# Half of w_in kept on chip until its split, half through DRAM once, and matmul operands moved to multiples of 2 KB

## The chip, the cores and the metric

The kernel runs on one core of a Trainium2 chip. The metric is the device time of one execution in microseconds. The engines are named as in the profile: PE (TensorE matmul, PEld its weight loads), DVE (VectorE), ACT (ScalarE), POOL (GpSimd) and SP (SyncE, which issues most DMAs).

## The reference

Three layers follow one another, all in f32 (some of the 64-bit inputs are cut to f32 on the chip).

```
attention, B=8, H=8, S=576, D=64: k and v pooled over 8 rows (72 keys);
  attn = softmax(q k_p^T / 8);  x = attn v_p, as 4608 tokens x 512
experts: e = argmax(x w_gate); gate = softmax(x w_gate)[e]; eom = sigmoid(x w_output_gate)
  x = gate * eom[e] * (relu(x w1[e]) w2[e])         8 experts, 512 -> 1024 -> 512
dense:   h = x w_in                                  512 -> 2048
         out = (s * relu(h)^2 + b) w_out             2048 -> 512
```

The change concerns w_in, 512 x 2048, and the places of the tiles that PE reads.

## The kernel before

**Precision.** Matmuls of the experts and of the dense layer run on f32r operands. To keep f32 accuracy an operand is split into hi (ACT: a copy that rounds, L800) and lo (DVE: the rest, L801), by `split`, and each product is three matmuls: hi hi, hi lo, lo hi.

**Stages.** Attention runs to about 222 us, the experts to about 742, the dense layer from 749.8 to the end. The experts go slot by slot (128 tokens of one expert, 39 slots here): `l1` (L996, 24 matmuls, weights xh and xl, moving operand wa), a transpose, `l2` (L1025, 24 matmuls, moving operand wb). In each slot the function `side` also calls `db.step`, which prepares the dense layer's weights. The dense layer runs over 9 groups of 512 tokens, and in each over 16 blocks f of 128 hidden units: `c1(g, f)` (L1222, 12 matmuls, weights a block of 128 columns of wa or wb, moving operand xdh and xdl), relu on ACT, square and affine on DVE, a split into gh (ACT) and gl (DVE), and two steps later `c2(g, f)` (L1251, four times 3 matmuls, one for each 128 tokens j, weights gh and gl, moving operand wo[f]) into the four accumulators po0 to po3. After the last f of a group `store` copies each po to a yo tile (ACT for even, DVE for odd tokens' blocks) and POOL sends it out by an indirect DMA. A step below is one c1 and one c2: 24 matmuls. Program order on each engine is the order written; nothing is reordered.

**w_in and w_out.** They come in as 64-bit numbers. `Doubles` turns them into f32 in 64 pieces of 128 rows by 256 columns: a load (SP), then in `step` (L909) a pipeline of three calls per piece over ACT, DVE and POOL, whose last operation is POOL's add (L938), and a split. Pieces 0 to 11 and 44 to 63 are w_out's, 12 to 43 w_in's. The first 44 run beside the experts; the last 20 of w_out in steps 1 to 11 of dense group 0, two a step. A split piece of w_out goes to the wo tiles. A split piece of w_in, hi and lo, is stored to two DRAM tensors wi (64 stores of 128 KB), since wa and wb hold the experts' weights until the end of the experts. Then `reload` (L1371) brings them back into wa (columns 0 to 1023, in `tail`, 8 DMAs, 4 MB) and wb (columns 1024 to 2047, in steps 0 to 3 of group 0, two DMAs of 512 KB each).

**tail** (L1414) runs ahead of the last l2: it frees the experts' raw weights, opens the pool of xdh and xdl in their place, issues the reload of wa and the first two loads of w_out, and cuts (splits) the four slices of group 0's input.

**Places.** Pools on the left grow upward from the constants, two pools on the right downward from the top. On the left wa begins at byte 22464 of each partition, which is 11 x 2048 - 64; every later tile there that PE reads as f32r (wb, wo, xh, xl, hh, hl, gh, gl) begins at a multiple of 2 KB less 64 bytes too, since all sizes from there on are multiples of 1 KB. On the right the raw weights, and after them xdh and xdl, begin at a multiple of 2 KB less 32 bytes (xdh at 196576 = 96 x 2048 - 32). A slice of weights is 128 columns, 512 bytes, a moving operand 512 columns, 2 KB.

Of the kernel before, what the change touches and what calls it, by code (L numbers as in the profile page):

```python
# [8 lines left out]
F32 = mybir.dt.float32  # L9
F32R = mybir.dt.float32r  # L10
BF16 = mybir.dt.bfloat16
F16 = mybir.dt.float16
I32 = mybir.dt.int32
# [3 lines left out]
ALU = mybir.AluOpType  # L17
# [9 lines left out]
DM = H * D  # L27
E = 8
FE = 1024
FF = 2048  # L30
P = 128
# [767 lines left out]
def split(nc, hi, lo, raw, eng=None):  # L799
    nc.scalar.activation(out=hi, in_=raw, func=AF.Copy)  # L800
    (eng or nc.vector).tensor_tensor(out=lo, in0=raw, in1=hi.bitcast(F32), op=ALU.subtract)  # L801
# [60 lines left out]
CW = 256  # L862
# [7 lines left out]
class Doubles:  # L870
# [3 lines left out]


    def __init__(self, tc, ctx, w_in, w_out, wi):
        self.nc, self.tc = tc.nc, tc
        self.p3 = ctx.enter_context(tc.tile_pool(name="db3", bufs=3))
        self.wi, self.wo = wi, []
        self.more(ctx, EARLY * CW // DM)  # L880
        self.src = [w.bitcast(I32) for w in (w_out, w_in)]
        out = [(0, r, c) for r in range(FF // P) for c in range(DM // CW)]
        self.pieces = out[:EARLY] + [(1, r, c) for c in range(FF // CW) for r in range(DM // P)] + out[EARLY:]
        self.x, self.t, self.stores = {}, {}, []
        self.run(0, EARLY + len(self.pieces) // 2)
# [23 lines left out]
    def step(self):  # L909
        nc, n = self.nc, self.n  # L910
        if n == self.end + 3:
            return
        self.n += 1
        while self.stores:
            d, t = self.stores.pop(0)
            nc.sync.dma_start(out=d, in_=t)
        self.load(n + AHEAD)
        if n < self.end:
            x = self.x[n]
            t = self.p3.tile([P, CW], I32, tag="dt", name="dt", bufs=4)  # L920
            self.t[n] = t
            lo = x[:, :, 0]
            nc.scalar.activation(out=lo, in_=lo.bitcast(U32), func=AF.Copy, scale=2.0 ** -29)  # L923
            nc.vector.tensor_single_scalar(out=t, in_=x[:, :, 1], scalar=0x7FFFFFFF, op=ALU.bitwise_and)
            nc.gpsimd.tensor_scalar(
                out=t.bitcast(F32), in0=t.bitcast(F32), scalar1=LO64, scalar2=HI64, op0=ALU.max, op1=ALU.min
            )
        m = n - 1
        if self.begin <= m < self.end:
            x, t = self.x[m], self.t[m]  # L930
            nc.vector.tensor_scalar(
                out=t, in0=t, scalar1=3, scalar2=0x3FFFFFFF,
                op0=ALU.logical_shift_left, op1=ALU.bitwise_and,
            )
            nc.vector.scalar_tensor_tensor(  # L935
                out=t, in0=x[:, :, 1], scalar=-0x40000000, in1=t, op0=ALU.bitwise_and, op1=ALU.bitwise_or
            )
            nc.gpsimd.tensor_tensor(out=t, in0=t, in1=x[:, :, 0], op=ALU.add)  # L938
        m = n - 2
        if self.begin <= m < self.end:  # L940
            x, f = self.x.pop(m), self.t.pop(m).bitcast(F32)
            w, r, c = self.pieces[m]
            if w == 0:
                hi, lo = [o[:, c * CW:(c + 1) * CW] for o in self.wo[r]]
            else:
                hi = x.rearrange("p c w -> p (c w)")[:, 0:CW].bitcast(F32R)
                lo = f.bitcast(F32R)
            split(nc, hi, lo, f)
            if w == 1:
                for d, s in zip(self.wi, (hi, lo)):  # L950
                    self.stores.append((d[:, r, c * CW:(c + 1) * CW], s.bitcast(F32)))


def experts(ctx, tc, c, kp, wt, xd, ys, wide, side, ahead, tail):
# [212 lines left out]
class Dense:  # L1167
# [43 lines left out]
    def run(self, ctx, reload):  # L1211
        nc, tc, xs, gs, po, s_b = self.nc, self.tc, self.xs, self.gs, self.po, self.s_b
        db = self.db
# [49 lines left out]
                store(GT * g + j, o)  # L1263

        def store(t, src):
            y = p3.tile([P, DM], F32, tag="yo", name="yo", bufs=4)
            if t % 2:
                nc.vector.tensor_copy(out=y, in_=src)
            else:
                nc.scalar.copy(out=y, in_=src)  # L1270
            nc.gpsimd.indirect_dma_start(  # L1271
                out=self.out[:, :], out_offset=bass.IndirectOffsetOnAxis(ap=self.tok.to[:, t:t + 1], axis=0),
                in_=y, in_offset=None,
            )
# [5 lines left out]
        for n in range(len(steps)):  # L1280
            nxt = None
            g, f = steps[n]
            if g > 0 and g + 1 < NGRP and f % 2 == 0:
                k = f % 8 // 2
                if f < 8:
                    self.load(g + 1, k)
                else:
                    self.join(g + 1, k, [nc.gpsimd, nc.gpsimd])
                    nxt = g + 1, k
            if g == 0 and REST < f <= REST + 4:  # L1290
                nxt = 1, f - REST - 1
                self.join(*nxt, [nc.scalar, nc.vector])
            rest = g == 0 and 1 <= f <= REST
            c1(g, f, db.step if rest else None)
            if rest:
                db.step()
            if g == 0:
                if f < 4:
                    reload(f)
                if f == REST:  # L1300
                    for k in range(4):
                        self.load(1, k)
            if LAG <= n < len(steps) - END + LAG:
                g, f = steps[n - LAG]
                for j in range(GT):
                    c2(g, f, f + 1, j)
            if nxt is not None:
                self.cut(*nxt)
# [5 lines left out]
def kernel(  # L1314
# [15 lines left out]
    nc = tc.nc  # L1330
    ctx.enter_context(tc.manual_schedule())
    c = constants(tc, ctx, nc)
# [12 lines left out]

    ys = dram.tile([N + P, 2 * DM], U16, name="ys")
    tok = Tokens(nc, kpool, dram.tile([N, 2], I32, name="tab"), dram.tile([N, 1], F32, name="gsd"))
    wi = [dram.tile([P, DM // P, FF], F32, name=f"wi{i}") for i in range(2)]

    wt = Experts(tc, moe_w1, moe_w2, kpool)  # L1350
    raw = ExitStack()
    for i in range(2):
        wt.open_raw(i, raw.enter_context(tc.tile_pool(name=f"raw{i}", bufs=1, side="right")))
# [14 lines left out]
        attention(x, tc, c, q, k, v, moe_w_gate, moe_w_output_gate, xd, lg, ro, hooks)  # L1368
    wt.open_b(ctx.enter_context(tc.tile_pool(name="wb", bufs=1)))

    def reload(i, f0, f1):  # L1371
        for m, w in enumerate((wt.a, wt.b)[i]):
            nc.sync.dma_start(
                out=w.bitcast(F32).rearrange("p (k f) -> p k f", f=FE)[:, :, f0:f1],
                in_=wi[m][:, :, FE * i + f0:FE * i + f1],
            )

    db = Doubles(tc, ctx, moe2_w_in, moe2_w_out, wi)

# [31 lines left out]
                dn.join(0, k, [nc.scalar, nc.vector])  # L1411

    with ExitStack() as x:
        def tail():  # L1414
            raw.close()
            dn.open(ctx.enter_context(tc.tile_pool(name="dn2", bufs=2, side="right")))
            reload(0, 0, P)
            reload(0, P, 2 * P)
            db.run(db.end, len(db.pieces))
            reload(0, 2 * P, 4 * P)  # L1420
            reload(0, 4 * P, FE)
            for k in range(4):
                dn.cut(0, k)

        experts(x, tc, c, kp, wt, xd, ys, wide, side, ahead, tail)
    dn.run(ctx, lambda j: reload(1, 2 * P * j, 2 * P * (j + 1)))


_INS = [
# [23 lines left out]
```

## Time and profile before

| | us |
|---|---|
| median of 3 runs | 1573.66 |
| lowest, highest | 1565.76, 1579.52 |
| the profiled execution, own time | 1566.95 |
| its span (first to last instruction) | 1565.3 |
| PE busy | 1500.5 (96%) |
| DVE, ACT, POOL busy | 817.2, 527.9, 491.3 |

The span is what the profile covers; its own time includes 1.65 us around it. Busy times of engines overlap. A matmul's duration in the profile includes the way through the array, so it is longer than the distance from one start to the next; the distance is what counts, and it is read from starts.

### The profile page before, as it was taken

The numbers are of one execution on the slowest core, as the hardware profiler recorded it, in microseconds if no ns is written. First come the engines' busy times: TensorE is split into PE (matmuls) and PEld (weight loads), VectorE is DVE, ScalarE is ACT, GpSimd is POOL, SyncE is SP. The second block draws the span as 40 slices with busy tenths as digits, with TensorE's granted clock in tenths as the row PEclk, the third lists the DMA queues.
The fourth block names the chain that finished last, engine by engine and source line by source line (L and its number), as shares of the span: only waits on it lengthen the run. The fifth ranks groups of instructions, "written<-read, shape, count | busy, mean of one in ns | idle before, by whom it ended". The sixth has DMA issues, their size and how long they took to land.

```text
span 1565.3 us, 21155 instructions
## 1 busy us (share of the span) xinstructions
PE 1500.5 (96%) x7280; PEld 1226.6 (78%) x7280; DVE 817.2 (52%) x1516; ACT 527.9 (34%) x1017; POOL 491.3 (31%) x521
## 2 busy tenths in 40 slices
PE   5998999999989999998999999999999999999997
PEld 4876878887768887886887888888888888888885
DVE  6688775576644657433695434343444434444332
ACT  3554524254433345222343222222222222222221
POOL 6745222355554454500460304040220404040000
PEclk8999999999989999999999999999999999999999
DMA  8975244255744647492923101010010101000000
GB/s 243 262 233 150 82 135 176 69 185 156 235 164 104 204 132 235 132 83 57 308 71 77 28 14 41 21 41 21 27 34 14 35 14 41 14 27 1 23 5 27
DMA packets 139592, 153.56 MB, mean 98 GB/s; under 512 B 62078, under 2 KB 96126, under 8 KB 139454
## 3 DMA queue, kind: packets, MB, share of 16 engines
q1 hardware_dynamic: 123918, 101.83, 23.4%
q0 software_dynamic: 15536, 50.12, 10.3%
q8 instruction: 59, 0.97, 0.3%
q14 instruction: 79, 0.65, 0.2%
HBM read 104.93 MB, written 37.54 MB: 91 GB/s over the span
## 4 chain that ended last, share of the span: by engine, by line
PE 46%; DVE 3%; DMA 1%; ACT 1%; SPq 1%; issue 1%; POOLq 0%; DVEq 0%; ACTq 0%
PE po L1259 8%; PE ph L1228 8%; PE ph L1230 8%; PE ph L1229 8%; PE po L1261 8%; PE po L1260 7%; DVE gl L1248 1%; DVE r L1234 1%; DMA dx<-in_moe_w_out 1%; DVE r L1233 0%; PE py L1034 0%; DVE wo L801 0%; DVE dt L935 0%; ACT dx L923 0%; DVE dy L1201 0%
## 5 line engine op out<-in xcount | busy, mean ns | idle before, releaser
L1233 DVE TENSOR_TENSOR r<-r 128x512 f32<-128x512 f32 x144 | 104.9, 728 | 320.8 <-ACT r L1232 320.6
L1271 POOL DMA_INDIRECT out<-yo,kp_pos x36 | 35.7, 991 | 604.0 <-ACT yo L1270 523.2
L1259 PE MATMUL po<-wo,gh 128*128 128x512 f32 x560 | 221.9, 396 | 0.0
L1261 PE MATMUL po<-wo,gl 128*128 128x512 f32 x560 | 219.8, 393 | 0.0
L1260 PE MATMUL po<-wo,gh 128*128 128x512 f32 x560 | 218.1, 389 | 0.0
L1034 PE MATMUL py<-wb,hh 128*128 128x512 f32 x624 | 196.1, 397 | 10.8 <-ACT wb L800 6.2
L1232 ACT ACTIVATE r<-ph 128x512 f32<-128x512 f32 x144 | 85.9, 597 | 342.8 <-PE ph L1230 342.8
L1245 ACT ACTIVATE gh<-r 128x512 fp32r<-128x512 f32 x140 | 88.6, 633 | 213.0 <-DVE r L1234 213.0
L1248 DVE TENSOR_TENSOR gl<-r,gh 128x512 fp32r<-128x512 f32 x140 | 106.4, 760 | 90.7 <-ACT gh L1245 90.7
L1034 PEld LDWEIGHTS py<-wb,hh 128*128 128x128 f32 x624 | 119.5, 192 | 38.6 <-ACT wb L800 6.6
L1004 PE MATMUL ph<-wa,xh 128*128 128x512 f32 x312 | 122.7, 393 | 4.1 <-DVE wa L801 4.0
L1003 PE MATMUL ph<-wa,xh 128*128 128x512 f32 x312 | 125.7, 403 | 0.0
L1261 PEld LDWEIGHTS po<-wo,gl 128*128 128x128 f32 x560 | 105.3, 188 | 26.0 <-DVE gl L1248 0.3
L1260 PEld LDWEIGHTS po<-wo,gh 128*128 128x128 f32 x560 | 105.6, 189 | 24.4
L1259 PEld LDWEIGHTS po<-wo,gh 128*128 128x128 f32 x560 | 105.4, 188 | 23.1
L1005 PE MATMUL ph<-wa,xl 128*128 128x512 f32 x312 | 122.1, 391 | 0.0
L1034 PE MATMUL py<-wb,hl 128*128 128x512 f32 x312 | 121.4, 393 | 0.0
L1228 PE MATMUL ph<-xdh,wa 128*128 128x512 f32 x288 | 114.3, 397 | 1.8 <-ACT xdh L800 1.8
L1230 PE MATMUL ph<-xdh,wa 128*128 128x512 f32 x288 | 114.3, 397 | 0.0
L1228 PE MATMUL ph<-xdh,wb 128*128 128x512 f32 x288 | 114.2, 396 | 0.0
L1229 PE MATMUL ph<-xdl,wa 128*128 128x512 f32 x288 | 113.8, 395 | 0.3 <-DVE xdl L801 0.3
L1230 PE MATMUL ph<-xdh,wb 128*128 128x512 f32 x288 | 114.0, 396 | 0.0
(231 smaller groups left out, 2739.2 us busy)
## 6 DMA issues: line engine op xcount, KB each, us to landing
wr<-in_moe_w POOLq DMA_DIRECT2D x56, 512.0 KB
ys<-y SPq DMA_DIRECT2D x38, 256.0 KB
xd<-x SPq DMA_DIRECT2D x36, 256.0 KB
q<-in_q SPq DMA_DIRECT2D x16, 512.0 KB
vr<-in_v SPq DMA_DIRECT2D x8, 1024.0 KB
wr<-in_moe_w SPq DMA_DIRECT2D x16, 512.0 KB
dx<-in_moe_w_out SPq DMA_DIRECT2D x32, 256.0 KB
dx<-in_moe_w_in SPq DMA_DIRECT2D x32, 256.0 KB
```

Source lines behind the costliest of these rows:

```text
L1003: nc.tensor.matmul(ph, lhsT=xh[:, k], rhs=wh[:, k, s], start=k == 0, stop=False)
L1004: nc.tensor.matmul(ph, lhsT=xh[:, k], rhs=wl[:, k, s], start=False, stop=False)
L1005: nc.tensor.matmul(ph, lhsT=xl[:, k], rhs=wh[:, k, s], start=False, stop=k == 3)
L1034: nc.tensor.matmul(py, lhsT=a, rhs=w, start=j == 0, stop=j == len(steps) - 1)
L1228: nc.tensor.matmul(ph, lhsT=wh[:, k, s], rhs=xh[:, k], start=k == 0, stop=False)
L1229: nc.tensor.matmul(ph, lhsT=wh[:, k, s], rhs=xl[:, k], start=False, stop=False)
L1230: nc.tensor.matmul(ph, lhsT=wl[:, k, s], rhs=xh[:, k], start=False, stop=k == 3)
L1233: nc.vector.tensor_tensor(out=r, in0=r, in1=r, op=ALU.mult)
L1248: nc.vector.tensor_tensor(out=gl, in0=r, in1=gh.bitcast(F32), op=ALU.subtract)
L1259: nc.tensor.matmul(o, lhsT=gh[:, s], rhs=wh, start=f == 0, stop=False)
L1260: nc.tensor.matmul(o, lhsT=gh[:, s], rhs=wl, start=False, stop=False)
L1261: nc.tensor.matmul(o, lhsT=gl[:, s], rhs=wh, start=False, stop=f == NC - 1)
```

## The change

The adds of w_in's first 1024 columns write straight into a tile wf (128 x 4 x 1024, f32, 16 KB a partition) that lives beside the experts' tiles; they are split into wa by `front` in `tail`, in three parts of 256, 384 and 384 columns (128x1024, 128x1536, 128x1536 elements). The pieces of the other 1024 columns are stored once, as f32 (16 stores of 128 KB), into one DRAM tensor. `reload(j)` in steps 0 to 3 of group 0 loads 256 columns (512 KB) into wb's lo tile, and in steps 1 to 4 splits what the step before has loaded: hi from it, lo in place. No w_in piece is split beside the experts any more. 64 bytes of padding stand ahead of wa, 2016 bytes at the top of the right side, so that both sides' tiles begin at multiples of 2 KB; yo has three buffers in place of four.

```diff
--- before.py
+++ after.py
@@ -874,9 +874,10 @@
 
 
     def __init__(self, tc, ctx, w_in, w_out, wi):
+
         self.nc, self.tc = tc.nc, tc
         self.p3 = ctx.enter_context(tc.tile_pool(name="db3", bufs=3))
-        self.wi, self.wo = wi, []
+        self.wi, self.wo, self.wf = wi, [], None
         self.more(ctx, EARLY * CW // DM)
         self.src = [w.bitcast(I32) for w in (w_out, w_in)]
         out = [(0, r, c) for r in range(FF // P) for c in range(DM // CW)]
@@ -912,8 +913,8 @@
             return
         self.n += 1
         while self.stores:
-            d, t = self.stores.pop(0)
-            nc.sync.dma_start(out=d, in_=t)
+            c, r, t = self.stores.pop(0)
+            nc.sync.dma_start(out=self.wi[:, r, c * CW - FE:(c + 1) * CW - FE], in_=t)
         self.load(n + AHEAD)
         if n < self.end:
             x = self.x[n]
@@ -935,20 +936,18 @@
             nc.vector.scalar_tensor_tensor(
                 out=t, in0=x[:, :, 1], scalar=-0x40000000, in1=t, op0=ALU.bitwise_and, op1=ALU.bitwise_or
             )
-            nc.gpsimd.tensor_tensor(out=t, in0=t, in1=x[:, :, 0], op=ALU.add)
+            w, r, c = self.pieces[m]
+            o = self.wf[:, r, c * CW:(c + 1) * CW].bitcast(I32) if w == 1 and c * CW < FE else t
+            nc.gpsimd.tensor_tensor(out=o, in0=t, in1=x[:, :, 0], op=ALU.add)
         m = n - 2
         if self.begin <= m < self.end:
-            x, f = self.x.pop(m), self.t.pop(m).bitcast(F32)
+            self.x.pop(m)
+            f = self.t.pop(m).bitcast(F32)
             w, r, c = self.pieces[m]
             if w == 0:
-                hi, lo = [o[:, c * CW:(c + 1) * CW] for o in self.wo[r]]
-            else:
-                hi = x.rearrange("p c w -> p (c w)")[:, 0:CW].bitcast(F32R)
-                lo = f.bitcast(F32R)
-            split(nc, hi, lo, f)
-            if w == 1:
-                for d, s in zip(self.wi, (hi, lo)):
-                    self.stores.append((d[:, r, c * CW:(c + 1) * CW], s.bitcast(F32)))
+                split(nc, *[o[:, c * CW:(c + 1) * CW] for o in self.wo[r]], f)
+            elif c * CW >= FE:
+                self.stores.append((c, r, f))
 
 
 def experts(ctx, tc, c, kp, wt, xd, ys, wide, side, ahead, tail):
@@ -1263,7 +1262,7 @@
                 store(GT * g + j, o)
 
         def store(t, src):
-            y = p3.tile([P, DM], F32, tag="yo", name="yo", bufs=4)
+            y = p3.tile([P, DM], F32, tag="yo", name="yo", bufs=3)
             if t % 2:
                 nc.vector.tensor_copy(out=y, in_=src)
             else:
@@ -1295,7 +1294,7 @@
             if rest:
                 db.step()
             if g == 0:
-                if f < 4:
+                if f < 5:
                     reload(f)
                 if f == REST:
                     for k in range(4):
@@ -1345,9 +1344,12 @@
 
     ys = dram.tile([N + P, 2 * DM], U16, name="ys")
     tok = Tokens(nc, kpool, dram.tile([N, 2], I32, name="tab"), dram.tile([N, 1], F32, name="gsd"))
-    wi = [dram.tile([P, DM // P, FF], F32, name=f"wi{i}") for i in range(2)]
-
+    wi = dram.tile([P, DM // P, FF - FE], F32, name="wi")
+
+
+    kpool.tile([P, 16], F32, name="pad0")
     wt = Experts(tc, moe_w1, moe_w2, kpool)
+    ctx.enter_context(tc.tile_pool(name="top", bufs=1, side="right")).tile([P, 504], F32, name="pad1")
     raw = ExitStack()
     for i in range(2):
         wt.open_raw(i, raw.enter_context(tc.tile_pool(name=f"raw{i}", bufs=1, side="right")))
@@ -1368,12 +1370,21 @@
         attention(x, tc, c, q, k, v, moe_w_gate, moe_w_output_gate, xd, lg, ro, hooks)
     wt.open_b(ctx.enter_context(tc.tile_pool(name="wb", bufs=1)))
 
-    def reload(i, f0, f1):
-        for m, w in enumerate((wt.a, wt.b)[i]):
-            nc.sync.dma_start(
-                out=w.bitcast(F32).rearrange("p (k f) -> p k f", f=FE)[:, :, f0:f1],
-                in_=wi[m][:, :, FE * i + f0:FE * i + f1],
-            )
+    def columns(w, f0, f1):
+        return w.rearrange("p (k f) -> p k f", f=FE)[:, :, f0:f1]
+
+    def front(f0, f1):
+
+        split(nc, *[columns(w, f0, f1) for w in wt.a], db.wf[:, :, f0:f1])
+
+    def reload(j):
+
+        if j < 4:
+            s = 2 * P * j, 2 * P * (j + 1)
+            nc.sync.dma_start(out=columns(wt.b[1], *s).bitcast(F32), in_=wi[:, :, s[0]:s[1]])
+        if j > 0:
+            hi, lo = [columns(w, 2 * P * (j - 1), 2 * P * j) for w in wt.b]
+            split(nc, hi, lo, lo.bitcast(F32))
 
     db = Doubles(tc, ctx, moe2_w_in, moe2_w_out, wi)
 
@@ -1411,19 +1422,20 @@
                 dn.join(0, k, [nc.scalar, nc.vector])
 
     with ExitStack() as x:
+        db.wf = x.enter_context(tc.tile_pool(name="wf", bufs=1)).tile([P, DM // P, FE], F32, name="wf")
+
         def tail():
             raw.close()
             dn.open(ctx.enter_context(tc.tile_pool(name="dn2", bufs=2, side="right")))
-            reload(0, 0, P)
-            reload(0, P, 2 * P)
+            front(0, 2 * P)
             db.run(db.end, len(db.pieces))
-            reload(0, 2 * P, 4 * P)
-            reload(0, 4 * P, FE)
             for k in range(4):
                 dn.cut(0, k)
+            front(2 * P, 5 * P)
+            front(5 * P, FE)
 
         experts(x, tc, c, kp, wt, xd, ys, wide, side, ahead, tail)
-    dn.run(ctx, lambda j: reload(1, 2 * P * j, 2 * P * (j + 1)))
+    dn.run(ctx, reload)
 
 
 _INS = [
```

## Rows read from the trace of the kernel before

**Rows 1.** The page, 40 equal slices: tenths of busy time, granted clock

```profile
PE   5998999999989999998999999999999999999997
...
PEclk8999999999989999999999999999999999999999
```

**Rows 2.** Busy time by stage: stretch, its length, each engine, clock, DMA

```profile
235.00:742.00 507.00, 483.07 (x2320) 398.62 (x2319) 274.82 (x470) 198.70 (x349) 208.21 (x221) 0.98 0.53 149
749.60:838.40 88.80, 86.82 (x372) 69.25 (x370) 72.13 (x146) 37.46 (x81) 42.23 (x40) 1.00 0.56 173
838.40:1551.00 712.60, 712.50 (x3069) 576.84 (x3070) 291.63 (x430) 180.38 (x301) 130.10 (x146) 1.00 0.08 24
```

**Rows 3.** Timeline of PE, one dense step: start, length, instruction

```profile
876.74 0.40 PE L1228 MATMUL ph<-xdh,wa 128*128 128x512 f32 x1
...
879.54 0.40 PE L1259 MATMUL po<-wo,gh 128*128 128x512 f32 x1
...
880.94 0.39 PE L1259 MATMUL po<-wo,gh 128*128 128x512 f32 x1
...
882.30 0.40 PE L1228 MATMUL ph<-xdh,wb 128*128 128x512 f32 x1
```

**Rows 4.** Timeline of PE, an l2 of the experts, first and last

```profile
732.86 0.61 PE L1034 MATMUL py<-wb,hh 128*128 128x512 f32 x2
...
737.62 0.62 PE L1034 MATMUL py<-wb,hh 128*128 128x512 f32 x2
```

**Rows 5.** Timeline of PE after the stall at 836

```profile
839.38 0.63 PE L1259 MATMUL po<-wo,gh 128*128 128x512 f32 x1
...
841.51 0.63 PE L1261 MATMUL po<-wo,gl 128*128 128x512 f32 x1
```

**Rows 6.** Timeline of PE, the run-out

```profile
1544.72 0.40 PE L1259 MATMUL po<-wo,xdh 128*128 128x512 f32 x1
...
1546.82 0.39 PE L1259 MATMUL po<-wo,gh 128*128 128x512 f32 x1
...
1547.96 0.40 PE L1261 MATMUL po<-wo,gl 128*128 128x512 f32 x1
```

**Rows 7.** Timeline of PE in attention, and line 275 (ns, least, median, most)

```profile
147.46 1.15 PE L275 MATMUL sc<-kbd,qT 128*128 128x144 f32 x8
...
L275 PE MATMUL sc<-kbd,qT x256: 286/286/448, 15.0 to 204.5; 128*128 128x144 f32 x128
```

**Rows 8.** Lines 801 and 800 by form: busy us, mean ns, idle before

```profile
L801 DVE TENSOR_TENSOR wb<-wr,wb 128x1024 fp32r<-128x1024 f32 x32 | 39.7, 1295 | 11.0 <-ACT wb L800 9.9 <-DMA wr<-in_moe_w 1.0
...
L800 ACT ACTIVATE wb<-wr 128x1024 fp32r<-128x1024 f32 x32 | 31.7, 1051 | 15.1 <-DMA tab<-tok,kp_pos 6.6 <-DVE dt L935 4.1 <-DMA wr<-in_moe_w 3.3
```

**Rows 9.** Timeline of DVE, first dense group

```profile
755.43 0.69 DVE L1248 TENSOR_TENSOR gl<-r,gh 128x512 fp32r<-128x512 f32 x1 [0.70 <-ACT gh L1245]
...
765.70 0.29 DVE L924 TENSOR_SCALAR dt<-dx 128x256 int32<-128x256 int32 x1 [4.32 <-DMA dx<-in_moe_w_out]
...
772.79 1.23 DVE L1248 TENSOR_TENSOR gl<-r,gh 128x512 fp32r<-128x512 f32 x1
```

**Rows 10.** Chain of waits in order of time: start, length

```profile
774.46 0.60 DVE dt L935
...
814.94 0.60 DVE dt L935
```

**Rows 11.** Timelines of DVE, POOL and PE at a group's end

```profile
938.62 1.28 DVE L1268 COPY yo<-po 128x512 f32<-128x512 f32 x2
...
938.73 1.02 POOL L1271 DMA_INDIRECT out<-yo,kp_pos  x1 [61.41 <-ACT yo L1270]
...
943.88 1.23 POOL L1271 DMA_INDIRECT out<-yo,kp_pos  x1 [4.12 <-DVE r L1234]
...
942.78 0.39 PE L1259 MATMUL po<-wo,gh 128*128 128x512 f32 x1
```

**Rows 12.** Waits of DVE beside the experts: us, times, longest

```profile
DVE dt L924 <- DMA wi<-dt: 18.0, 5, 7.3
```

## The prediction

> **What bounds the kernel now.** I read the page's slices first: PE is busy in nearly all of them and its granted clock stands at the upper of its two levels, 2.4 GHz, but for a few slices [rows 1]. The table by stage says the same in microseconds: from 838.4 on PE is busy 712.50 of 712.60 us, in the experts' stage 483.07 of 507.00, in the first group of the dense layer 86.82 of 88.80 [rows 2]. So the time is set by how far apart matmuls start, and I went to PE's timeline for that. In a step of the dense layer the twelve matmuls of c1 take 879.54 - 876.74 = 2.80 us, 233 ns each; the first six of c2 take 1.40 us, 233 ns; its last six take 1.36 us, 227 ns; the step 5.56 us [rows 3]. Twenty-one matmuls of l2 take 737.62 - 732.86 = 4.76 us: 227 ns [rows 4]. After a stall, at the lower clock (1.2 GHz), five take 841.51 - 839.38 = 2.13 us, 426 ns [rows 5]; half of that, 213 ns, is what 512 columns take at the upper clock. Every matmul thus starts 14 to 20 ns later than its columns ask for, and this gap, not an idle engine, is what there is to win.
>
> **What the gap hangs on.** c1 and l1 have the same order of operands and differ in the place of the moving one: c1 reads xdh and xdl, which begin 32 bytes short of a multiple of 2 KB; l1, l2 and c2 read tiles that begin 64 bytes short. In the run-out nine matmuls that take xdh and xdl as weights, with wo as moving operand, take 1546.82 - 1544.72 = 2.10 us, 233 ns; the next five, with gh and gl as weights and the same wo, take 1547.96 - 1546.82 = 1.14 us, 228 ns [rows 6]. So a start that is 32 bytes off costs about 6.7 ns, whichever of the two operands has it. 6.7 ns is 16 columns, or 64 bytes of a row. The 227 that is left lies 13.3 above 213.3, two such steps, and both operands of every such matmul still begin 64 bytes off. Matmuls of plain f32 show next to none of it: eight passes of 144 columns take 1.15 us, the last of them 0.286, so (1.15 - 0.286) / 7 = 123 ns each, 3 more than 144 columns at half the pace of the others (2 x 213.3 / 512 = 0.833 ns a column) [rows 7].
>
> **Part by part, against the profiled execution** (span 1565.3, own time 1566.95; it lies 6.7 us below the median of the three runs, so I carry the difference over to the median).
>
> The offsets. With 64 bytes more ahead of wa and 2016 bytes at the top, every operand of these matmuls begins on a multiple of 2 KB, or for weight slices of 512 bytes. Bounds for the start-to-start time: 227 ns for all (only c1 and the start of c2 after it gain), and 213.3 + 3 = 216 ns (only the few ns of rows 7 stay). I take 216, since the two steps of 6.7 ns add up to just what is left and a step is what an offset costs in rows 6. Of the 144 steps, 128 lie after 838.4 (712.6 / 128 = 5.57 us [rows 2]). Each becomes 24 x 0.216 = 5.18 instead of 5.56: 128 x 0.376 = **-48**; at 227 it is 24 x 0.2267 = 5.44, 128 x 0.12 = -15. The experts' 39 slots of 48 matmuls: 1872 x 0.0107 = 20, of which I take **-18**, as PE waits for others there for 24 us [rows 2] and some gain goes into those waits; at 227 it is 0.
>
> The rule for this on the page TensorE: Matmul & The Clock Gate of the Trainium skill (Back-to-back issue gap) is columns / 2.4 plus 2.5 ns, 215.7 for 512 columns, and it knows no address. The trace disagrees as the operands lie now, with 227 and 233 [rows 3, 4]; by the rule alone, were it met after the change, the sum would be 1 to 2 us below mine. The page SBUF — State Buffer of the Trainium skill (Operand start alignment) asks of an f32 operand a multiple of 4 bytes and calls that legality, not speed; rows 6 show that speed does hang on the start.
>
> The first dense group. There c1's and c2's gain is not on the path: the chain runs through DVE, with 5.78 us a step ((814.94 - 774.46) / 7 [rows 10]) against PE's 5.56, and PE waits at its end for the cut of the next group. DVE gets the front splits and the splits of reload. A split of 128x1024 takes 1.295 us on DVE after 1.051 on ACT [rows 8]. Fronts are 128x1024 and twice 128x1536, 4 x 1.295 = 5.2 on DVE, all in tail ahead of its first step. They fall where DVE now idles 4.32 us for the loads of w_out [rows 9], which queue behind 8 reload DMAs (4 MB) on SP; these go, and with them the wait. The first split of reload, in step 1, adds up to 1.3 there; I count the whole stretch to 765.7 as even. The splits in steps 2 to 4 come on top: three times 1.3, or 2.3 where DVE waits for ACT's half: 3.9 to 7, I take **+4.5**. Bounds: 0 if the fronts can start sooner than the cut does now, 10 if none of the 5.2 is covered.
>
> What waits behind the fronts: the cut of group 0, behind the first of them only, so 1.3 us later. It ends just ahead of PE now, and PE needs a slice of it each 0.7 us, so I cost this at nothing, at most 1.3, as the last l2 covers the first slice. The copies of the last slot's y come behind all three fronts, some 4 us later; the next reader of ys is the load of group 1, in step 11: nothing. The new wo tiles lie where wf was, so the first split of w_out waits for the fronts: they are through some 10 us ahead of it. On SP, reload issues one DMA a step instead of two, ahead of the next loads of w_out: a gain that is in the wait above.
>
> What would cost more there: DVE's subtraction gl takes 0.69 us at 755.43 with POOL idle and 1.23 at 772.79 beside POOL's work [rows 9]. The page SBUF — State Buffer of the Trainium skill (Who interferes with whom) says that a VectorE instruction with two SBUF inputs and a GpSimd one that reads SBUF block each other; the row agrees. By it each of the three splits could wait for one more operation of POOL; that is inside the bound of 10.
>
> The output's buffers, four to three. At a group's end four copies go to four yo tiles, and POOL sends them one at a time: starts at 938.73 and 943.88 [rows 11]. The fourth copy, on DVE, ran in 938.62 to 939.90; it now waits until the first tile has been sent, by 943.88 at the latest, and takes 0.64. It empties po3, which PE wants at 942.78 for the next group. So PE waits up to 943.88 + 0.64 - 942.78 = 1.7 us, eight times; nothing if the tile is read out a microsecond and a half sooner. Queued behind the copy on DVE are r and gl of the next step, which PE needs only two steps later. I take 1.2, and 0.2 more as a faster PE comes earlier: 8 x 1.4 = **+11**; bounds 0 and 15.
>
> The experts' stage loses 32 splits of 128x256 on ACT and DVE and 48 of 64 stores. DVE waits 18.0 us for landing stores there [rows 12]; PE feels little of it: **-3**, bounds -8 and +1. Nothing is costed for the one store that each piece of the second half keeps, on SP, and for POOL's add, which only writes elsewhere.
>
> Sum: -48 - 18 + 4.5 + 11 - 3 = -53.5; 1566.95 becomes 1513, the median 1573.66 becomes **1520**.
>
> **Rivals.** *The gap is a constant of these matmuls at 64 bytes and more*, and only the 32 bytes counted: 227 for all. For it: the same 227 for l1, l2 and c2 with weight slices at all four multiples of 512 less 64, so nothing shows that a larger offset matters. Then -15.4 + 4.5 + 9.5 - 3 = -4.4: 1569, bounds 1550 to 1588. *Half of it goes* (one operand's step): 220 ns, -36 - 12 + 4.5 + 10 - 3 = -36: 1537. *Slower: the yo wait.* At 1.7 us, or more if the next group's chain slips with it, eight group ends cost 14, the first group 4.5, and nothing is won if offsets do nothing for reading and c1 is slow for another cause: 14 + 4.5 - 3 = +15.5: 1589. It decides once the step gains less than (14 + 4.5 - 3) / 128 = 0.12 us, which is what 227 for all would give. *The change doesn't do what it says*: the offsets follow from tile sizes that are all multiples of 1 KB, so I fold the little chance of this into the last case.
>
> **Chances.** Forecast 0.42 (own range 1506 to 1534, its bounds not all met at once), half 0.08, constant gap 0.36, slower 0.14. The range reaches from 1506 to 1577, which takes in three quarters of the constant gap. Measurements of this kernel can't tell a change under about 1%: faster than 1558 in the first two and a little of the third, 0.52; within 1% for most of the third and half of the last, 0.37; slower than 1589, 0.11.
>
> **What would show it.** Right: c1, c2, l1 and l2 all at 216 ns, the step at 5.2 us; wrong: 227 throughout (5.44), or c1 still at 233. The first group right: no wait of DVE for w_out's loads, a step of about 7 us while splits run, PE waiting there for DVE. The yo wait right: DVE's fourth copy 4 us late and a gap of about 1.4 us on PE ahead of the tenth matmul of each group's first c2; wrong: no gap. The forecast falls if weights and moving operands at like multiples get into each other's way and the 227 rises.

## The result and the profile after

The changed kernel takes 1558.71 us (median of 7 runs, 1553.79 to 1562.89), the kernel before, run beside it, 1574.52 (7 runs, 1565.76 to 1579.52). The ratio is 0.9912, 95% interval 0.9891 to 0.9934: some 14 us off, where 54 were forecast. The profiled execution of after is the slowest of its seven (1562.89, span 1561.3) and that of before lies low among its own, so the two spans are only 4 us apart; I compare stages, and what a stage is worth in the kernel as a whole by the ratios of the runs.

Busy time by stage (stretch, its length, then each engine's busy time, clock, DMA): the experts, the first dense group, the rest, against [rows 2].

```profile
238.00:749.00 511.00, 483.88 (x2321) 399.06 (x2321) 265.11 (x438) 188.37 (x317) 208.83 (x221) 0.99 0.50 136
755.90:840.90 85.00, 83.41 (x362) 67.06 (x361) 76.49 (x143) 39.79 (x83) 43.44 (x40) 1.00 0.37 107
840.90:1547.00 706.10, 700.71 (x3080) 577.12 (x3079) 296.51 (x438) 182.72 (x305) 129.42 (x146) 1.00 0.09 25
```

In the last stretch before, PE was idle 0.1 of 712.6 us; now it is idle 5.4 of 706.1. 2.6 of that is the wait for group 1's cut, at 843, which before lay in the stretch ahead; the other 2.8 is new. The experts' PE time, 483.9 us, is what it was (483.1; the two stretches are 511 and 507 us long).

PE's timeline of one dense step, against [rows 3]: the twelve matmuls of c1 take 885.20 - 882.48 = 2.72 us, each half of c2 1.36, the step 5.44. That is 227 ns throughout; the 233 of c1 and of the first half of c2 are gone, and nothing below 227 has come.

```profile
882.48 0.39 PE L1227 MATMUL ph<-xdh,wa 128*128 128x512 f32 x1
...
885.20 0.39 PE L1258 MATMUL po<-wo,gh 128*128 128x512 f32 x1
...
886.56 0.39 PE L1258 MATMUL po<-wo,gh 128*128 128x512 f32 x1
...
887.92 0.39 PE L1227 MATMUL ph<-xdh,wb 128*128 128x512 f32 x1
```

PE's timeline of the last full l2, against [rows 4]: 743.33 - 738.57 = 4.76 us for 21 matmuls, to the hundredth what it was, though every operand now begins on a multiple of 512 bytes.

```profile
738.57 0.62 PE L1033 MATMUL py<-wb,hh 128*128 128x512 f32 x2
...
743.33 0.62 PE L1033 MATMUL py<-wb,hh 128*128 128x512 f32 x2
```

A group's end in the timelines of DVE, POOL and PE, against [rows 11]. The second copy on DVE (the fourth of the group) no longer follows the first; it waits 3.25 us for the first tile to be sent. PE, which wants the accumulator that this copy empties, starts its next matmul 0.90 us after the one at 1034.20 instead of 0.23.

```profile
1030.42 0.68 DVE L1267 COPY yo<-po 128x512 f32<-128x512 f32 x1
1034.36 0.69 DVE L1267 COPY yo<-po 128x512 f32<-128x512 f32 x1 [3.25 <-DMA out<-yo,kp_pos]
...
1030.53 1.02 POOL L1270 DMA_INDIRECT out<-yo,kp_pos  x1 [61.92 <-ACT yo L1269]
1034.93 0.97 POOL L1270 DMA_INDIRECT out<-yo,kp_pos  x1 [3.37 <-DMA out<-yo,kp_pos]
...
1034.20 0.39 PE L1260 MATMUL po<-wo,gl 128*128 128x512 f32 x1
1035.10 0.50 PE L1258 MATMUL po<-wo,gh 128*128 128x512 f32 x1 [0.51 <-DVE yo L1267]
```

DVE's timeline in the first dense group shows the four splits of w_in's reload, of which the first and the last stand here, one a step and (787.36 - 765.93) / 3 = 7.1 us apart. Then PE runs out of work: 1.78 us lie between two starts at 791.5, and 0.40 to 0.44 once in each of five steps after it, where 0.23 is usual.

```profile
765.93 1.21 DVE L801 TENSOR_TENSOR wb<-wb,wb 128x1024 fp32r<-128x1024 f32 x1
...
787.36 1.21 DVE L801 TENSOR_TENSOR wb<-wb,wb 128x1024 fp32r<-128x1024 f32 x1
```

From the first matmul of the dense layer to its last, before takes 805.1 us and after 795.0. Group by group, from first c1 to first c1: 83.8 became 85.0, the second 93.1 became 90.6, the six after it 88.96 became 87.4 to 87.9, and what comes behind the last of these 94.4 became 92.9. Some 1.6 us of the second group's gain are the clock's: behind the wait for the cut, before ran some eight matmuls at the 1.2 GHz level [rows 5], and after none. The program of after up to its last c2 stands in two more profiles below, the two benches, and its dense layer takes 797.7 us (with 6.8 us at the lower clock in the second group) and 794.3 there; so a length read from one profile is good to some 3 us. The other 4 of the 14 us show in no row: over the profiles of this study the stretch from the first l1 to the first c1 is 510 to 517 us long (522.7 in the one with matmuls added ahead of the first c1), with no order in it that goes with a change.

### The profile page after: what moved, and what is told of

The parts are those of the page before. It is cut to its first block, busy times and chain, and to the rows that moved or that the text cites. A ratio compares the mean times of both kernels' runs of the same rounds, so it can differ in the third digit from the quotient of the medians.

```text
span 1561.3 us, 21038 instructions
## 1 busy us (share of the span) xinstructions
PE 1485.9 (95%) x7280; PEld 1224.8 (78%) x7280; DVE 819.8 (53%) x1491; ACT 525.1 (34%) x992; POOL 492.5 (32%) x521
## 3 DMA queue, kind: packets, MB, share of 16 engines
q0 software_dynamic: 15536, 50.12, 10.1%
## 4 chain that ended last, share of the span: by engine, by line
PE 42%; DVE 5%; DMA 2%; ACT 1%; issue 1%; SPq 0%; another core or an unknown queue 0%; POOLq 0%; ACTq 0%; DVEq 0%
PE ph L1228 7%; PE ph L1229 7%; PE ph L1227 7%; PE po L1258 7%; PE po L1259 7%; PE po L1260 7%; DMA out<-yo,kp_pos 2%; DVE r L1232 1%; DVE gl L1247 1%; DVE r L1233 1%; DVE wo L801 0%; DVE wb L801 0%; ACT gh L1244 0%; DVE yo L1267 0%; ACT yo L1269 0%
## 5 line engine op out<-in xcount | busy, mean ns | idle before, releaser
L1232 DVE TENSOR_TENSOR r<-r 128x512 f32<-128x512 f32 x144 | 108.7, 755 | 282.0 <-ACT r L1231 281.8
L1247 DVE TENSOR_TENSOR gl<-r,gh 128x512 fp32r<-128x512 f32 x140 | 107.0, 764 | 90.6 <-ACT gh L1244 90.6
L1227 PE MATMUL ph<-xdh,wa 128*128 128x512 f32 x288 | 112.2, 390 | 2.3 <-ACT xdh L800 2.3
L1229 PE MATMUL ph<-xdh,wa 128*128 128x512 f32 x288 | 112.1, 389 | 0.0
L1227 PE MATMUL ph<-xdh,wb 128*128 128x512 f32 x288 | 112.0, 389 | 0.0
L1228 PE MATMUL ph<-xdl,wb 128*128 128x512 f32 x288 | 112.0, 389 | 0.0
```

What stands on the lines that cost most here:

```text
L1227: nc.tensor.matmul(ph, lhsT=wh[:, k, s], rhs=xh[:, k], start=k == 0, stop=False)
L1228: nc.tensor.matmul(ph, lhsT=wh[:, k, s], rhs=xl[:, k], start=False, stop=False)
L1229: nc.tensor.matmul(ph, lhsT=wl[:, k, s], rhs=xh[:, k], start=False, stop=k == 3)
L1232: nc.vector.tensor_tensor(out=r, in0=r, in1=r, op=ALU.mult)
L1247: nc.vector.tensor_tensor(out=gl, in0=r, in1=gh.bitcast(F32), op=ALU.subtract)
```

## The experiments

**Each half alone.** The new way of w_in alone is after with both pads taken out and four yo buffers:

```
-            y = p3.tile([P, DM], F32, tag="yo", name="yo", bufs=3)
+            y = p3.tile([P, DM], F32, tag="yo", name="yo", bufs=4)
-    kpool.tile([P, 16], F32, name="pad0")
-    ctx.enter_context(tc.tile_pool(name="top", bufs=1, side="right")).tile([P, 504], F32, name="pad1")
```

> The changed kernel with both paddings taken out and four yo tiles again: w_in's new way alone, tiles where they were before. If the places carry the gain (theory): c1 back at 233 ns a matmul, a step of 5.57 us, no wait for yo at a group's end; first dense group 85 to 87 us (before 83.8, DVE's added splits); in all within 5 us of the kernel before, ratio 0.998 to 1.004. If w_in's new way carries it (rival: fewer splits and stores beside the experts): steps of 5.57 us all the same, but 8 us or more gone from the experts' stage, ratio 0.990 to 0.995.

Measured: ratio 0.9981 (0.9963 to 0.9998). c1 at 233.6 ns and c2 at 229.8 in the mean, as before; the first dense group 87.3 us where before has 83.8, the second 93.0, the others 88.96 as before, no yo wait. So the new w_in costs 3.5 us in the first group, near the 4.5 of the forecast, and by the ratio as much and more comes back elsewhere; no row shows where.

The places alone are before with the two pads and three yo buffers:

```
-            y = p3.tile([P, DM], F32, tag="yo", name="yo", bufs=4)
+            y = p3.tile([P, DM], F32, tag="yo", name="yo", bufs=3)
+    kpool.tile([P, 16], F32, name="pad0")
+    ctx.enter_context(tc.tile_pool(name="top", bufs=1, side="right")).tile([P, 504], F32, name="pad1")
```

> The kernel before with the two paddings and three yo tiles, w_in handled as before: the places alone. If the places carry the gain: 227 ns throughout, a step of 5.44 us, group ends with a wait of 0.4 to 1.1 us ahead of c2's tenth matmul, groups 1 to 7 at 87.8 us against 88.96; 128 x 0.12 = 15 less 8 x 0.75 = 6 for yo, so 9 to 10 us gone, ratio 0.993 to 0.995, and the first dense group little changed, as DVE bounds it. If w_in's new way carries it: ratio 0.998 to 1.001, as the yo wait eats what the step gives.

Measured: 0.9991 (0.9975 to 1.0007). The ratio expected was missed, and that of the rival was met, so this run alone doesn't tell who carries the gain. All dense matmuls are at 226.8 ns, but the groups still take 88.2 to 90.8 us: ahead of the tenth matmul of each group's first c2, 1.2 to 2.7 us lie between two starts. The two halves, 0.2% and 0.1%, don't add up to the 0.9% of both together. So something else joins them, and it is in the yo wait, which is twice as long here as in after.

**Which start counts.** Are multiples of 64 bytes enough, or must it be 2 KB? After with no pad on the left, 32 bytes at the top of the right side, and four yo buffers. Every operand of these matmuls then begins 64 bytes short of a multiple of 512.

```
-    kpool.tile([P, 16], F32, name="pad0")
-    ctx.enter_context(tc.tile_pool(name="top", bufs=1, side="right")).tile([P, 504], F32, name="pad1")
+    ctx.enter_context(tc.tile_pool(name="top", bufs=1, side="right")).tile([P, 8], F32, name="pad1")
-            y = p3.tile([P, DM], F32, tag="yo", name="yo", bufs=3)
+            y = p3.tile([P, DM], F32, tag="yo", name="yo", bufs=4)
```

> The changed kernel without the padding ahead of wa, with 32 bytes at the top in place of 2016, and with four yo tiles: every operand at a multiple of 64 bytes, 64 short of a multiple of 2 KB. If 32 bytes off a multiple of 64 is all that costs (theory): 227 ns throughout as in the changed kernel, no wait for yo, groups 1 to 7 at 87.1 us, 5 to 6 us faster than the changed kernel, ratio to the kernel before 0.986 to 0.990. If a multiple of 2 KB is what the right side needs (rival): c1 at 230 to 233 ns, steps of 5.5 us and more, ratio 0.995 or more.

Measured: 1550.26 us, ratio 0.9883 (0.9862 to 0.9903), the lowest median of all. 226.7 ns everywhere, and the groups from the third on take 87.04 us, 16 times 5.44; PE is busy all of the stretch from the wait for the cut to the run-out. The multiples of 2 KB buy nothing that 32 bytes don't.

```profile
840.00:1532.00 692.00, 692.00 (x3055) 573.19 (x3054) 290.10 (x427) 179.60 (x300) 129.37 (x146) 1.00 0.08 25
```

Then the left pad cut to 32 bytes, so that the operands on the left begin 32 bytes short of a multiple of 2 KB and xdh and xdl, on the right, on one:

```
-    kpool.tile([P, 16], F32, name="pad0")
+    kpool.tile([P, 8], F32, name="pad0")
```

> The changed kernel with 32 bytes of padding ahead of wa in place of 64: all operands on the left 32 bytes past a multiple of 64, xdh and xdl still at a multiple of 2 KB. If each operand's own start counts (theory): l1, l2 and c2, both operands off, at 233 to 240 ns; c1, weights off, at 233; the whole slower than the kernel before, by 10 to 40 us. If what counts is that the two operands of a matmul start differently (rival): l1, l2 and c2 at 227, c1 at 233, and about the kernel before's time with the yo wait on top.

Measured: 0.9995 (0.9971 to 1.0019). PE's timelines of an l2, both of whose operands are 32 off, and of a c1, whose weights alone are:

```profile
732.60 0.61 PE L1033 MATMUL py<-wb,hh 128*128 128x512 f32 x2
...
737.36 0.62 PE L1033 MATMUL py<-wb,hh 128*128 128x512 f32 x2
...
888.53 0.40 PE L1227 MATMUL ph<-xdh,wb 128*128 128x512 f32 x1
...
891.34 0.40 PE L1258 MATMUL po<-wo,gh 128*128 128x512 f32 x1
```

l2 takes 4.76 us for 21, 227 ns as ever; c1 takes 2.81 for twelve, 234. A start that is 32 bytes off costs nothing if the other operand's is off alike. The reading of [rows 6] on which the forecast stood, that each operand's own start has its price, falls.

**Why the yo wait differs.** In the records of the DMA queues, one 16 KB transfer of instructions falls near each group's end, always at the same place: a group has 384 matmuls with a weight load each, 768 instructions, and there are three such transfers a group. That the code is PE's follows from a count: there are 59 of these transfers in before and after, 60 with the 128 instructions that are added below, 63 with the some 1000 of a bench. In before and in the places alone it starts 1.5 to 2.6 us after the first out DMA was issued, while that DMA's packets move; in after 0.7 to 1.0 us after, mostly ahead of them. To move it and nothing else, I put 64 small matmuls ahead of the first dense step of the places alone:

```
+        for i in range(64):
+            if i % 32 == 0:
+                sh = psh.tile([P, GT * P], F32, tag="ph", name="shift")
+            w = self.w[0][0]
+            nc.tensor.matmul(sh[:, 0:64], lhsT=w[:, 0:P], rhs=w[:, 0:64], start=i % 32 == 0, stop=i % 32 == 31)
```

> The places alone (e2), with 64 small matmuls of 64 columns ahead of the first dense step, whose sum nobody reads: 128 more instructions in TensorE's program, and nothing else. In e2 and in before, TensorE's code comes in transfers of 16 KB, three to a group of 768 instructions, and one of the three starts 1.5 to 2.6 us after each group's first out DMA was issued, while that DMA's packets go out; the next out DMA starts 5.4 us after the first in the mean. After, e1, e3 and e4 have that transfer at 0.7 to 1.0 us and 4.0 to 4.5 us. Theory: that meeting makes the first out DMA late, and so the long yo wait of e2; 128 instructions move it by half a transfer, some 14 us away. Then the second out DMA starts 3.4 to 3.9 us after the first, the wait of PE ahead of the tenth matmul of a group's first c2 falls from 1.2 to 2.7 us to under 0.5, the third and later groups fall from 88.2 to 90.8 us to 87.0 to 87.5, and with 3 to 5 us for the small matmuls the ratio to before is 0.990 to 0.995. Rival: the new way of w_in shortens the out DMA by something else (its smaller DRAM tensor, less traffic): the gap stays 5.2 to 5.6 us, the wait stays, ratio 1.001 to 1.004.

Measured: 0.9922 (0.9899 to 0.9946), 11 us faster than the places alone, by work that is added: the dense layer takes 786.4 us in place of 806.9, and the stretch ahead of it is 11 us longer. The second out DMA starts 3.5 to 3.6 us after the first, and the groups from the third on take 87.04 to 87.09 us. What waited for DVE's copies of po (the view of that one line: idle time before it, then who waited for it, us and times), in the places alone:

```profile
  DMA out<-yo,kp_pos: 34.1, 8
...
  PEld po L1259: 15.5, 8
  PE po L1259: 12.1, 8
```

The same view with the code moved:

```profile
  DMA out<-yo,kp_pos: 19.0, 8
...
  PEld po L1259: 0.3, 1
```

The same view of after:

```profile
  DMA out<-yo,kp_pos: 24.8, 8
...
  PEld po L1258: 6.2, 8
  PE po L1258: 2.8, 6
```

And the DMA engines from the first out DMA's issue to the second's (40 slices of that stretch, tenths of busy share; then the queues: packets, MB, share of 16 engines), in the places alone:

```profile
DMA  0000000000869896000000010010000000000000
...
q8 instruction: 1, 0.02, 2.0%
```

The same with the code moved:

```profile
DMA  0000000000000000009899797100000000000000
q0 software_dynamic: 80, 0.26, 18.2%
```

The same in after:

```profile
DMA  0000000006000057999910001000000000000000
...
q8 instruction: 1, 0.02, 1.6%
```

The stretches last 5.61, 3.53 and 4.40 us. In the first the instructions and the output leave together, and packets still move in the 24th and the 27th slice, 3.2 to 3.8 us after the issue (the last one ends at 4.4); in the second there is no such transfer; in the third it shows by itself in the 10th slice, ahead of the output. That the transfer meets the output is shown to be what makes the yo wait long. That it comes some 0.8 us sooner in after fits a count in the traces: PE's queue holds 162 semaphore instructions in after and 157 in before, and five instructions at some 113 ns (half of 227) are 0.57 us. This last link I didn't test by itself, and it is not shown.

**The places without the yo wait.** Before with 32 bytes at the top of the right side and nothing else:

```
+    ctx.enter_context(tc.tile_pool(name="top", bufs=1, side="right")).tile([P, 8], F32, name="pad1")
```

> Before with nothing but 32 bytes put at the top of the right side, so that both operands of every dense matmul start alike modulo 64 bytes; w_in goes the old way and yo keeps 4 buffers. Theory (only the two operands' difference counts, and e2 lost its gain to the yo wait): c1 and c2 at 226.8 ns, no yo wait, the second and later groups at 87.0 to 87.2 us in place of 88.96, the run-out 16 x 6.7 ns shorter, in all some 14 to 16 us: ratio 0.990 to 0.991, nearly all that e3 gains. Rival (the gain of e3 needs w_in's new way beside the places): pitch 226.8 ns but a ratio of 0.996 to 1.001, as e2.

Measured: 1554.04 us, 0.9888 (0.9842 to 0.9933). Busy time in one stretch, the third to the eighth group: PE is busy all of 522.20 us, six groups of 87.03. The second group, with the wait for the cut in it, still takes 91.6.

```profile
927.00:1449.20 522.20, 522.20 (x2305) 432.42 (x2304) 222.57 (x324) 136.43 (x229) 107.56 (x120) 1.00 0.09 25
```

The dense layer takes 789.7 us from first matmul to last, 15.4 less than before, with one short fall of the clock in each. The code meets the output here too (the second out DMA starts 5.0 to 5.9 us after the first), but with four tiles nothing waits for it. One line of 32 bytes thus gives as much as the whole change, within the intervals, and a dense layer that is 5 us shorter; beside it the new way of w_in gives nothing that can be measured (0.9883 with it, 0.9888 without, intervals that overlap).

**What the 227 is made of.** Series of matmuls behind after's last c2. In an even series both operands begin on multiples of 512 bytes; in the others the moving operand (m), the weights (w) or both begin some bytes further on. A time that a series settles at is the mean of its last twelve or so.

```
+        def series(name, n, w0=0, m0=0, wide=512, same=False, dt=F32R, banks=1):
...
+                nc.tensor.matmul(
+                    o[i % banks][:, 0:wide], lhsT=ws[:, w0 + u:w0 + u + P], rhs=mv[:, m0:m0 + wide],
+                    start=i < banks, stop=i >= n - banks,
+                )
```

> After with 23 series of 24 matmuls each behind its last c2, sums that nobody reads: f32r, 128x128 weights from w_in's first half, moving from its second; even starts; moving 16, 32, 48, 64, 96, 128 bytes off; weights 16, 32, 64 off; both 32 and both 16 off; 256 columns (even, and 32 off), 384 columns; the same weights all the time (even, and 32 off); two banks by turns; bf16 (even, and 32 off); even again. Theory (difference of the two starts modulo 64): 227 ns for even, 64 and 128 off, both 32 and both 16 off; 233 ns for moving or weights 32 off and for 96. For 16 and 48 it has no value of its own, between 227 and 240. Rival (each operand's own start): both 32 off at 233 or 240. What is left above 213.3 ns (512 columns at 2.4 GHz): if it belongs to each matmul as a constant, 256 columns take 120 ns and 384 take 173; if to the columns, 113.4 and 170; if to changing the weights, the series with the same weights takes 213 to 216; if to f32r, bf16 takes 213 to 216; if to adding to one bank, two banks do.

PE's timeline (series of like names are merged; the time of one matmul is from a row's start to the next row's, over its count):

```profile
1548.02 5.60 PE L1320 MATMUL even<-wb,wa 128*128 128x512 f32 x24
1553.46 33.64 PE L1320 MATMUL m<-wb,wa 128*128 128x512 f32 x144
1586.93 16.94 PE L1320 MATMUL w<-wb,wa 128*128 128x512 f32 x72
1603.71 11.19 PE L1320 MATMUL both<-wb,wa 128*128 128x512 f32 x48
1614.74 3.04 PE L1320 MATMUL n<-wb,wa 128*128 128x256 f32 x24
1617.62 3.00 PE L1320 MATMUL n256m<-wb,wa 128*128 128x256 f32 x24
1620.45 4.33 PE L1320 MATMUL n<-wb,wa 128*128 128x384 f32 x24
1624.62 5.64 PE L1320 MATMUL same<-wb,wa 128*128 128x512 f32 x24
...
1635.70 5.64 PE L1320 MATMUL banks<-wb,wa 128*128 128x512 f32 x24
1641.18 5.35 PE L1320 MATMUL bf<-dy 128*128 128x512 bf16 x23
```

Even: 5.44 / 24 = 226.7 ns. 256 columns: 2.88 / 24 = 120.0, which is 106.7 at 2.4 GHz and 13.3; 384 columns settle at 173.3, which is 160 and 13.3. With even starts the gap is thus a constant of each f32r matmul and doesn't grow with its columns; that it isn't the offsets' either, the run with 64 bytes shows, with 226.7 for starts 64 bytes short. It stays with the same weights all the time (226.7 once settled) and with two banks by turns (226.9); it goes with bf16 (one of its 24 records is missing), whose matmuls settle at 215.8 with even starts and with the moving operand 32 off. The rule that the forecast weighed, in the Trainium skill's page TensorE: Matmul & The Clock Gate (Back-to-back issue gap), columns / 2.4 plus 2.5 ns, thus agrees with bf16 here to the tenth; for f32r 13.3 stands in place of its 2.5. The same section of the Trainium skill calls this the gap of an isolated matmul and gives about 131 ns for 512 columns in a stream of weight loads and matmuls. The series here are such streams, and none of 512 columns comes below 215.8.

The weights' rows fell out of the theory: 16.78 / 72 = 233 ns for all three, 64 bytes off too, where a difference modulo 64 would be zero; moving 128 off also took 233. Both 32 off settled at 226.7, both 16 off at 231. So a second bench, with longer series and more differences:

```
+        for d in (64, 128, 256, 512, 1024, 2048):
+            series(f"m{d}", 32, m0=d // 4)
+        for d in (128, 256):
+            series(f"w{d}", 32, w0=d // 4)
+        for d in (16, 48, 64, 128, 256):
+            series(f"both{d}", 32, w0=d // 4, m0=d // 4)
```

> After with 14 series of 32 f32r matmuls of 512 columns behind its last c2, sums that nobody reads. In the bench before (e7) weights and moving operands both 32 bytes off took 227.2 ns, but weights 64 off alone 233.4, moving 64 off 228.8 and 128 off 233.4, and both 16 off 231.1. So the difference of the two starts must be a multiple of more than 64 bytes; of 512 it always is in the even series, whose weights lie 512 bytes apart. Series: even; moving 64, 128, 256, 512, 1024, 2048 bytes off; weights 128, 256 off; both 16, 48, 64, 128, 256 off; even again. Theory (the difference modulo 512 decides, and a start of its own counts only below 32 bytes): 227 ns for moving 512, 1024 and 2048 off and for both 64, 128 and 256 off; 233 for moving 64, 128, 256 off and weights 128 and 256 off; both 16 off at 231. Rival (modulo 256): moving and weights 256 off at 227. Rival (a start must be a multiple of 64 and nothing else; what came out in e7 is left behind by the uneven series ahead of it): moving 128 and weights 128 off at 227 behind the even ones.

PE's timeline, the last 21 matmuls of some series: even, moving 128, 256 and 512 off, weights 128 and 256 off, both 48 and both 128 off (the time of one is the length less the 0.39 of the last, over 20):

```profile
1542.44 4.92 PE L1318 MATMUL even<-wb,wa 128*128 128x512 f32 x21
...
1557.10 5.04 PE L1318 MATMUL m<-wb,wa 128*128 128x512 f32 x21
...
1564.52 4.92 PE L1318 MATMUL m<-wb,wa 128*128 128x512 f32 x21
...
1571.77 4.92 PE L1318 MATMUL m<-wb,wa 128*128 128x512 f32 x21
...
1593.61 5.04 PE L1318 MATMUL w<-wb,wa 128*128 128x512 f32 x21
1600.98 4.92 PE L1318 MATMUL w<-wb,wa 128*128 128x512 f32 x21
...
1615.67 5.06 PE L1318 MATMUL both<-wb,wa 128*128 128x512 f32 x21
...
1630.39 4.93 PE L1318 MATMUL both<-wb,wa 128*128 128x512 f32 x21
```

4.92 is 226.5 ns, 5.04 is 232.5, 5.06 is 233.5. The first rival, modulo 256, has it: 128 bytes of difference cost 6 ns, whichever operand has them, 256 cost nothing. Starts that are off alike cost nothing at 128, at 64 and 256 neither (at 32 in the first bench), but both 48 off take 233 and both 16 off 230. So, as far as tried: two starts that are multiples of 32 bytes and differ by a multiple of 256.

## Why the forecast was wrong

**The step that failed** is this one: "I take 216, since the two steps of 6.7 ns add up to just what is left and a step is what an offset costs in rows 6". The 13.3 that was left is a constant of the f32r matmul, as the 256 and 384 columns show; that it is twice 6.7 said nothing of its cause. The 3 ns that were to remain came from plain f32 [rows 7], another type, and the benches show that the type matters (2.5 for bf16). And [rows 6] held two matmuls that differ in two things: xdh as weights has another start than gh, but also another start than the moving wo. I read the first and it was the second. The rival that took 227 for all was right in the step, and the trace had the evidence in l2 and in the end of c2, which were at the lower value with both operands 64 bytes off. Measured without other edits (the 32 bytes in before), the places are worth 15.4 us in the dense layer, just the -15 that the prediction gave for 227, in place of -48; and the experts' matmuls 0 in place of -18, since their operands already differed by multiples of 512 bytes. The result lies outside the forecast's own range (1506 to 1534); that the stated range of 1506 to 1577 holds it is owed to the part that was added for this rival, not to the mechanism. The rival's own sum, 1569, was 10 above the result: yo cost less than it took (9.5), w_in less than its 4.5, and some 4 us are found in no row.

**That c1 would gain** was right, and so was the start of c2, though for another reason than the forecast's: not its operand's own 32 bytes, but how its two operands lie against each other. c2's first matmuls were slow before though their own starts are alike, because c1 ran ahead of them: with 32 bytes that change c1's operands alone, c2 is at 227 from its first on. The first bench has the same sequence: in before, c2 takes 241, 224, 231, 236, 228, 232, 231 and then 227 ns, and so does the series with two banks, which follows a series with the moving operand 32 off, as it is in c1. It is no rule for every change of starts: weights 256 off, behind weights 128 off, has one slow matmul, and both 128 off, behind a settled series with both 64 off, has ten; why, stays open.

**The first dense group** was right in kind and about in size: a step of 7.1 us while the splits run, no wait of DVE for w_out's loads, PE waiting for DVE. At an unchanged step (w_in alone) it costs 3.5 us against +4.5; some of it comes back at the group's end, where the step is shorter: with the shorter step and four yo tiles the first two groups take 175.3 us with the new w_in and 175.2 with the old, and the old one's have some 1.6 us of lower clock in them, the new one's none, so w_in costs some 1.7 there.

**The yo wait** was right in its mechanism, place and victim: the fourth copy is 3.25 us late, and PE stands ahead of the tenth matmul of each group's first c2. The size was off: 6.2 us over eight groups on PE's weight queue, and 5.2 between the dense layers of after and of the run with 64 bytes and four tiles (795.0 and 789.8), against +11. The price was taken from POOL's starts in before [rows 11], 5.15 us apart, and these held a meeting with PE's code that the other half of the change moved away: 4.3 us in the mean in after. With the old w_in it costs 15.5 on the weight queue, half a microsecond above the forecast's upper bound, and the dense layers with three and with four tiles lie 17.2 apart (806.9 and 789.7), two falls of the clock in the one and one in the other.

**The experts' stage**, -3 (between -8 and +1), can't be read from a profile. By the runs w_in alone is worth 3 us in all (0.3 to 6), though its dense layer is 3.3 longer, so by subtraction some 6 would lie elsewhere; which stage has them is not shown.

**The sum** with the measured terms: -15.4 for the places, +5.2 to 6.2 for yo, +1.7 for w_in and -1.6 for the clock that fell in before's second group and not in after's: -9 to -10 in the dense layer, as the profile has it (-10.1); the other 4 by the runs are found in no row. The 40 us that are missing from the forecast are 33 of the dense steps' and 18 of the experts', less what yo and the first group came out better by. The warning, that operands at like multiples might get into each other's way, was the wrong way round: like starts are what is fast.

## What to carry to other kernels

Before a change of places is costed by an offset's price, find two matmuls in the trace that differ in one operand's start alone, and ask of each whether the difference of the two starts moved too; here 32 bytes at one end of the memory gave as much as two pads, a buffer less and another way for w_in together. A residue that equals a whole number of known steps is not yet made of them: vary the columns, and see whether it grows. A buffer is only free if the transfer behind it lands in time, and that depends on what else moves just then, the engines' own instructions included; PE's program is worth a look where a wait recurs at the same place of every group.

## What the runs showed that was not expected

With even starts an f32r matmul of 128 x 128 weights costs 13.3 ns beside its columns (120.0 for 256, 173.3 for 384, 226.7 for 512), a bf16 one 2.5 (215.8 for 512). Starts that differ by 16 to 128 bytes add 2 to 7 ns to 512 columns of f32r and nothing to bf16 (32 bytes tried); with 256 columns the 32 bytes even took 2 ns off (117.8 against 120.0). Moving 64 off is a case between, 228.8, and weights 64 off, at 232.9, are not its mirror. Why any of these, stays open.

Instructions are traffic too: a 16 KB transfer of PE's code that meets an out DMA of 256 KB makes its last packets land up to 4.7 us after its issue, against 2.8 to 3.3 where it comes a microsecond sooner and 2.4 where there is none. Behind two of the long yo waits of the places alone (2.24 us between two starts at 936.6, 2.71 at 1471.3) the granted clock fell as well, and the next matmuls started 427 ns apart, the 1.2 GHz level.
